# Fused attention and gated feed-forward block: VectorE's order in the ramp written out, a pair of maxima and the filler weights moved, first normalisations by column blocks

## The chip, the cores and the metric

The kernel runs on one core of a Trainium2 chip. The metric is device microseconds of one execution; lower is better. Three executions of the kernel before took 1042.8, 1043.43 and 1046.78 us (median 1043.43).

## The reference

```python
x = A_x                                    # 1 x 2048 x 640, float32
xn = _layernorm(x)                         # (x - mean) / sqrt(var + 1e-5)
qkv = xn @ wqkv                            # 32 heads of 20
scores = q k^T * 20 ** -0.5                # causal, sliding window of 256
attention = softmax(scores) v @ wo
h = gelu(xn @ w_gate) * (xn @ w_up)        # 1728 wide
return x + attention + h @ w_down
```

Matrix products are done in three parts, with each operand split into a high part and the rest (names ending in h and l), to keep float32's precision.

## The kernel before, in words

The 2048 tokens are 16 tiles of 128, taken in four chunks of 512. The program has three stages: a ramp, the attention, and the feed-forward with the output products. The ramp and the first part of the attention are what the change touches.

**The ramp.** For each tile VectorE takes the statistics (`ln_stats`: two halves at L149 and L150, joined at L151). For a group of tiles it then forms the reciprocal root of the variance (`ln_sqrt` and `ln_rstd`: L156 on VectorE, L157 on ScalarE, L162 to L165 on VectorE) and normalises each tile in place (`ln_apply`, L169, one instruction over all 640 columns). TensorE transposes the tiles of a chunk in five column blocks of 128 (`turn`, L185), each into a PSUM bank. ScalarE copies a block as the high part `xh` (L193) and VectorE subtracts that from the bank to give the rest, `xl` (L194). The bank is free again after that. The letters of a string such as "xmxmx" give each block its pool of banks: x is a pool of two, m one of four. A third pool of two, `psd`, holds the projections (tag "dn").

Chunk 0 has its own code, `first_chunk`, in which the order of every engine is the order of the code, since it stands inside `tc.manual_schedule`. It works on two pairs of tiles: statistics, root, normalisation, transposes, copies (L352) and subtractions (L349), then the products with the weights for the first q and k rows (L356). A small copy on GpSimd (`hold`, L370) waits for a pair's last normalised tile, and GpSimd's subtraction for the low weights (L366) stands behind it. The two projections of chunk 0 go out through `save_qk`: ScalarE copies the bank to bf16 (L277), VectorE subtracts (L273, into `r`), ScalarE copies again (L255), GpSimd subtracts (L259), and SyncE stores the three parts to DRAM (L268).

Chunks 1 to 3 are a loop over `c` that follows. There the scheduler of the language orders the engines. `ln_scale` takes the statistics and normalises a chunk's four tiles, `ln_turn` transposes them, and in between lie the products for v (`proj_v`) and the projections of the first q and k rows (`proj_qk`). The activations' tiles `xi` have eight buffers, so the load of a tile waits for the transposes of the tile eight before it.

**The attention.** `attention` is written as slots, 14 to a unit of four heads by 512 queries, with the order of all engines as in the code. Each slot has a few pieces of the work on the unit (scores and exponentials, scores for the maxima, products with v), and a share of filler: the remaining projections and part of the feed-forward, which keep TensorE busy. `pull_max` takes the next pairs of row maxima from a stream that runs ahead of the exponentials: TensorE makes scores in two banks of the m pool (L512), VectorE adds the mask and takes the maximum (L522). Twelve steps ahead of slot 0 belong to the ramp of the attention; there the even ones take two pairs each. In the units slots 0, 5 and 9 take two pairs, slot 0 of later units takes two more, and slot 3 of the first unit two.

SyncE issues nearly all loads and stores and does so in order. `load_stack` loads the q and k stacks of the unit three ahead, the k stack at slot 9 and the q stack at slot 12, in six transfers each (L487). The filler loads its next weights where its own progress asks for them, in `load_qk` (L234) and `load_gu`, two transfers of 320 KB each. `split_later` copies them some fourteen slots later on ScalarE (L656) and makes the low part on GpSimd (L661).

Of the kernel before, what the change touches and what calls it, by code (L numbers as in the profile page):

```python
# [30 lines left out]
NS = 14  # L31
# [36 lines left out]
def block_kernel(ctx, tc, x, wqk, wv, wgu, wdo, wdl, out):  # L68
# [96 lines left out]
        nc.vector.scalar_tensor_tensor(rs, ve, 1.5, rs, op0=OP.add, op1=OP.mult)  # L165
        return rs

    def ln_apply(xi, mv, rs):
        nc.vector.tensor_scalar(xi, xi, mv[:, 0:1], rs, op0=OP.subtract, op1=OP.mult)  # L169

    def ln_scale(xs, lp, mv=None, begun=0):
        n = len(xs)
        mv = mv or lp.tile([128, n, 2], F32, name="mv4", tag="mv4", bufs=2)
        for i in range(begun, n):
            ln_stats(xs[i], mv[:, i, :], lp)
        rs = ln_rstd(*ln_sqrt(mv, n, lp), n, lp)
        for i, xi in enumerate(xs):
            ln_apply(xi, mv[:, i, :], rs[:, i:i + 1])

    def turn(k, xs, where):  # L180
        n = len(xs)
        pool, tag = {"x": (psx, "ex"), "m": (psm, "mx"), "o": (psm, "mx")}[where]
        ps = pool.tile([128, n * 128], F32, name="ps_t", tag=tag)
        for i in range(n):
            nc.tensor.transpose(ps[:, i * 128:(i + 1) * 128], xs[i][:, k * 128:(k + 1) * 128], ident)  # L185
        return ps

    def ln_turn(t0, xs, where="xmxmx"):
        n = len(xs)
        cs = slice(t0 * 128, (t0 + n) * 128)  # L190
        for k in range(KT):
            ps = turn(k, xs, where[k])
            nc.scalar.activation(xh[:, k, cs], ps, AF.Copy)  # L193
            nc.vector.tensor_tensor(out=xl[:, k, cs], in0=ps, in1=xh[:, k, cs].bitcast(F32), op=OP.subtract)  # L194

    acts = {}
    done = set()
# [27 lines left out]
    def behind(fn, *a):  # L225
# [3 lines left out]
        else:  # L229
            fn(*a)  # L230

    def load_qk(t):
        raw = wrp.tile([128, KT, 128], F32, name="wr", tag="wr")
        nc.sync.dma_start(raw, wqk[t])  # L234
        return raw

    def split_qk(raw):
        return split(wp, raw, [128, KT, 128], "wq", nc.gpsimd)
# [106 lines left out]
    def first_chunk(xs, wr0, wr5, prep, v0, lp):  # L345
        halves = slice(0, 256), slice(256, 512)

        def low(k, ps, cs):
            nc.vector.tensor_tensor(out=xl[:, k, cs], in0=ps, in1=xh[:, k, cs].bitcast(F32), op=OP.subtract)  # L349

        def high(k, ps, cs):
            nc.scalar.activation(xh[:, k, cs], ps, AF.Copy)  # L352

        def part(ps, w, r, cs, first=False, last=False, ks=range(KT)):
            for k in ks:
                nc.tensor.matmul(ps[:, cs], w[:, k, :], r[:, k, cs], start=first and k == 0,  # L356
                                 stop=last and k == KT - 1, skip_group_check=True)

        def high_qk(raw):
            wh = wp.tile([128, KT, 128], F32R, name="wqh", tag="wqh")  # L360
            nc.scalar.activation(wh, raw, AF.Copy)
            return wh

        def low_qk(raw, wh):
            wl = wp.tile([128, KT, 128], F32R, name="wql", tag="wql")
            nc.gpsimd.tensor_tensor(out=wl, in0=raw, in1=wh.bitcast(F32), op=OP.subtract)  # L366
            return wh, wl

        def hold(xi):
            nc.gpsimd.tensor_copy(one[:, 0:1], xi[:, 0:1])  # L370

        with tc.manual_schedule(engines=MANUAL | {mybir.EngineType.Pool}):
            mv = [lp.tile([128, 2, 2], F32, name="mv", tag="mv", bufs=2) for _ in range(2)]
# [18 lines left out]
            ln_apply(xs[2], mv[1][:, 0, :], rs[:, 0:1])  # L392
            ln_apply(xs[3], mv[1][:, 1, :], rs[:, 1:2])
# [36 lines left out]
            mv = lp.tile([128, 4, 2], F32, name="mv4", tag="mv4", bufs=2)  # L430
            for j in range(2):
                ln_stats(xs[8 + j], mv[:, j, :], lp)
        save_qk(5, 0, dn[1])
        return w0, w5, v0, mv

    v0 = []
    with tc.tile_pool(name="lp", bufs=1, side="right") as lp:
# [15 lines left out]
        w0, w5, v0, mv = first_chunk(xs, wr0, wr5, prep, v0, lp)  # L453
# [6 lines left out]
        for c in range(1, NC):  # L460
            if c > 1:
                ln_scale(xs[4 * c:4 * c + 4], lp, *((mv, 2) if c == 2 else ()))
            ln_turn(4 * c, xs[4 * c:4 * c + 4], "xmxmx" if c == NC - 1 else "xmxmm")
            if 1 < c < NC - 1:
                xs += [ln_load(t, lp) for t in range(4 * c + 4, 4 * c + 8)]
            if c == 1:
                for i in range(NQ):
                    for j in (0, 2):
                        nc.sync.dma_start(qs[i][SR + 2:64, j:j + 2].rearrange("p j t -> p (j t)"), ones[2:4])
            if c == 2:  # L470
                raws1 = [load_qk(1), load_qk(6)]
            if c < NC - 1:
                run(*[proj_v(v0, 4 * c - 4 + i, None if i % 2 else (psm, "mx")) for i in range(0 if c > 1 else 2, 4)])
                run(proj_qk(0, w0, c), proj_qk(5, w5, c))
# [165 lines left out]
    def load_gu(f):  # L640
        raws = []
        for i in range(2 if f < NF - 1 else 1):
            raw = wrp.tile([128, KT, 128], F32, name="wr", tag="wr")
            nc.sync.dma_start(raw, wgu[2 * f + i])
            raws.append(raw)
        return raws

    def split_gu(pools, raws):
# [174 lines left out]
    def attention():  # L823
# [8 lines left out]
        for i in range(12):  # L832
# [700 lines left out]
```

## Time and profile before

| | us |
|---|---|
| median of three executions | 1043.43 |
| the profiled execution | 1043.06 |
| its span, first to last instruction | 1041.3 |
| TensorE busy | 1031.8 |
| VectorE busy | 740.3 |
| ScalarE busy | 527.9 |
| GpSimd busy | 384.5 |

In the rows, PE is TensorE and PEld its weight loads, DVE is VectorE, ACT ScalarE, POOL GpSimd, and SPq SyncE's queue. L and a number is a line of the kernel before. A row of the timeline has the start, the length, the engine, the line and operation, the tile written and those read, the shape and a count; in brackets stands how long the engine was idle before and what ended that. Neighbouring instructions of one kind are merged in a row, and with matmuls the end of one overlaps the start of the next.

### The profile page before, as it was taken

How to read it: one execution, taken by the hardware profiler on the slowest of the kernel's cores; microseconds unless marked ns; L12 is line 12 of the kernel's file. 1: busy time of each engine (PE TensorE's matmuls, PEld its weight loads, DVE VectorE, ACT ScalarE, POOL GpSimd, SP SyncE). 2: the span in 40 equal slices, each digit the busy share in tenths (PEclk: the TensorE clock that was granted, in tenths of full speed). 3: DMA queues.
4: the chain of work that ended last, by engine and by line, in shares of the span. 5: the costliest groups of instructions: out<-in, count | busy, mean ns of one | idle time of the engine just before them, and what ended most of it. 6: DMA issues, size and time to landing. Idle time of an engine off the chain costs nothing.

```text
span 1041.3 us, 25568 instructions
## 1 busy us (share of the span) xinstructions
PE 1031.8 (99%) x9396; PEld 834.4 (80%) x9396; DVE 740.3 (71%) x2018; ACT 527.9 (51%) x1120; POOL 384.5 (37%) x623
## 2 busy tenths in 40 slices
PE   9999999999999999999999999999999999999998
PEld 8887666666777666666678888888888999999998
DVE  7855666677656576777736778776556888888887
ACT  4434766767666666666675322223324544333332
POOL 5122778988765787766461111101110000000000
PEclk9999999999999999999999999999999999999999
DMA  6642356564633455343325576673117874433333
GB/s 224 182 144 70 110 157 182 160 181 142 185 98 99 117 150 163 94 145 109 99 76 190 187 248 212 246 256 110 72 58 268 252 244 138 137 128 111 127 122 105
DMA packets 102150, 158.74 MB, mean 152 GB/s; under 512 B 14172, under 2 KB 55260, under 8 KB 102024
## 3 DMA queue, kind: packets, MB, share of 16 engines
q1 hardware_dynamic: 99640, 150.94, 45.7%
q10 hardware_dynamic: 2384, 6.16, 1.9%
q8 instruction: 74, 1.21, 0.5%
q14 instruction: 52, 0.43, 0.1%
HBM read 101.78 MB, written 54.92 MB: 150 GB/s over the span
## 4 chain that ended last, share of the span: by engine, by line
PE 92%; DVE 5%; DMA 1%; issue 1%; ACT 1%; SPq 0%; DVEq 0%; ACTq 0%
PE ps_g L977 24%; PE ps L1249 23%; PE ps_d L108 19%; PE ps_e L577 8%; PE ps_v L108 6%; PE ps_o L620 5%; PE ps_m L512 5%; DVE junk L522 2%; PE ps_g L108 1%; PE ps_d L356 1%; DVE xi L169 0%; DMA qs<-qd 0%; PE ps_t L185 0%; DVE st L150 0%; DVE xl L194 0%
## 5 line engine op out<-in xcount | busy, mean ns | idle before, releaser
L522 DVE CUSTOM_DVE_ANT_0 junk<-ps_m,mask 128x320 bf16<-128x320 f32 (+2 forms) x512 | 242.5, 474 | 132.1 <-PE ps_m L512 73.6
L579 ACT ACTIVATE P<-ps_e 128x512 f32<-128x512 f32 (+2 forms) x384 | 198.7, 572 | 65.3 <-PE ps_e L577 64.6
L1249 PE MATMUL ps<-wb,at 128*128 128x320 f32 x999 | 155.9, 309 | 0.0
L1249 PEld LDWEIGHTS ps<-wb,at 128*128 128x128 f32 x999 | 148.9, 188 | 0.2
L592 POOL TENSOR_SCALAR_AFFINE_SELECT P<-P 128x256 f32<-128x256 f32 (+1 forms) x192 | 94.7, 495 | 72.4 <-ACT P L579 71.6
L577 PE MATMUL ps_e<-qs,ks 124*128 124x128 bf16 (+2 forms) x704 | 118.3, 278 | 0.1
L108 PE MATMUL ps_d<-xl,wqh 128*128 128x512 f32 x310 | 98.5, 421 | 0.0
L108 PE MATMUL ps_d<-xh,wqh 128*128 128x512 f32 x310 | 98.3, 421 | 0.0
L108 PE MATMUL ps_d<-xh,wql 128*128 128x512 f32 x310 | 97.6, 418 | 0.0
L101 POOL TENSOR_TENSOR wql<-wr,wqh 128x640 fp32r<-128x640 f32 x12 | 19.2, 1607 | 195.4 <-PE ps_g L977 150.8
L1249 PE MATMUL ps<-wt,at 128*128 128x320 f32 x552 | 88.9, 309 | 0.0
L577 PEld LDWEIGHTS <-ks 124*128 124x128 bf16 x704 | 49.5, 98 | 49.0 <-issue 34.4
L1249 PEld LDWEIGHTS ps<-wt,at 128*128 128x128 f32 x552 | 82.9, 188 | 0.1
L595 POOL TENSOR_SCALAR_AFFINE_SELECT P<-P 128x512 f32<-128x512 f32 (+1 forms) x144 | 76.8, 542 | 16.3 <-ACT P L579 16.3
L1203 ACT ACTIVATE at<-ss 128x512 fp32r<-128x512 f32 x59 | 37.3, 632 | 83.3 <-DVE ss L1082 83.3
L620 PE MATMUL ps_o<-P,v 64*32 64x320 f32 (+4 forms) x2816 | 74.2, 347 | 0.0
L259 POOL TENSOR_TENSOR pt<-r,pt 128x512 bf16<-128x512 f32 x40 | 46.7, 1167 | 64.4 <-ACT pt L255 64.0
L620 PEld LDWEIGHTS ps_o<-P,v 64*32 64x32 f32 x2816 | 50.8, 106 | 21.5 <-issue 0.9
L512 PE MATMUL ps_m<-ks,qs 60*64 60x320 bf16 (+3 forms) x1472 | 64.0, 260 | 3.2 <-DMA qs<-qd 1.1
L108 PEld LDWEIGHTS ps_d<-xh,wql 128*128 128x128 f32 x310 | 56.0, 189 | 10.2 <-issue 1.3
L1006 ACT ACTIVATE hr<-hr 128x512 f32<-128x512 f32 x20 | 12.6, 632 | 101.6 <-DVE hr L980 101.6
L108 PEld LDWEIGHTS ps_d<-xh,wqh 128*128 128x128 f32 x310 | 56.0, 189 | 9.8 <-issue 1.6
(197 smaller groups left out, 1981.6 us busy)
## 6 DMA issues: line engine op xcount, KB each, us to landing
hd<-he SPq DMA_DIRECT2D x50, 256.0 KB
hr<-hd SPq DMA_DIRECT2D x48, 256.0 KB
wr<-wgu SPq DMA_DIRECT2D x27, 320.0 KB
qs<-qd SPq DMA_DIRECT2D x64, 120.0 KB
ks<-kd SPq DMA_DIRECT2D x64, 120.0 KB
xi<-x SPq DMA_DIRECT2D x16, 320.0 KB
qs<-qd SPq DMA_DIRECT2D x64, 80.0 KB
ks<-kd SPq DMA_DIRECT2D x64, 80.0 KB
```

The costliest lines, as they stand in the source:

```text
L108: nc.tensor.matmul(ps, a(k), b(k), start=n == 0, stop=n == 3 * nk - 1)
L259: nc.gpsimd.tensor_tensor(out=pt[:, l, :], in0=r, in1=pt[:, 1, :], op=OP.subtract)
L512: nc.tensor.matmul(ps[64 * h:64 * h + 64, col:col + w], q[rows, j, q0:q0 + 64], ks_, start=True, stop=True, tile_position=(64 * r, 64 * h))
L522: nc.vector.tensor_tensor_reduce(out=junk[:, 0:n], in0=ps[:, 320 - n:320], in1=mask[:, 320 - n:320], scale=1.0, scalar=NEG, op0=OP.add, op ...
L577: nc.tensor.matmul(ps[:, col:col + n], k[0:QROWS, j, kc:kc + 128], q[0:QROWS, j, q0:q0 + n], start=True, stop=True)
L579: nc.scalar.activation(pt[:, j, lo:hi], ps[:, lo:hi], AF.Exp, scale=SCALE)
L592: nc.gpsimd.affine_select(out=a, in_=a, pattern=[[0, n], [1, 128]], compare_op=OP.is_ge, fill=0.0, base=0, channel_multiplier=-1)
L595: nc.gpsimd.affine_select(out=a, in_=a, pattern=[[0, n], [-1, 128]], compare_op=OP.is_ge, fill=0.0, base=-1, channel_multiplier=1)
L620: nc.tensor.matmul(os[r][32 * j:32 * j + 32, qa:qb], v[rows, w0_:w0_ + 32], pt[rows, j, col + qa - q0:col + qb - q0], start=r not in begun ...
L977: nc.tensor.matmul(ps, i, j, start=first and n == 0, stop=n == len(work) - 1, skip_group_check=True)
L1203: nc.scalar.activation(hi[:, 3:7], s, AF.Copy)
L1249: nc.tensor.matmul(ps[bank][:, 0:HD], *work[bank][j], start=bank not in begun, stop=final[p, bank] == n and j == len(work[bank]) - 1, skip ...
```

## The change

It has four parts.

1. *VectorE's order in the ramp.* The loop over chunks 1 to 3 now stands inside a manual schedule for VectorE, and its pieces are put in a written order. The statistics of the first two tiles of the next chunk (`ln_begin`) are taken as soon as a chunk has been normalised. `ln_scale` takes only the other two and follows the transposes of the chunk before. The second projection of chunk 0 leaves in the middle of chunk 1's transposes. The last block of chunk 3's transposes goes to a bank of the projections' pool (letter d) instead of the x pool. Loads move with the pieces: the second of two filler weights ahead of the last four tiles.
2. *A pair of maxima sooner.* Step 11 of the attention's ramp takes two pairs, and slot 3 of the first unit none.
3. *Filler weights behind the q stack.* In slots 5 to 13 of a unit the filler's weight loads are put off to slot 13.
4. *First normalisations by column blocks.* The two pairs of tiles in chunk 0 are normalised in columns 0 to 255 and then 256 to 639: two instructions a tile.

The core of the diff:

```diff
+    def ln_apply(xi, mv, rs, cs=slice(0, D)):
+        nc.vector.tensor_scalar(xi[:, cs], xi[:, cs], mv[:, 0:1], rs, op0=OP.subtract, op1=OP.mult)
+
+    def ln_begin(xs, lp):
+        mv = lp.tile([128, 4, 2], F32, name="mv4", tag="mv4", bufs=2)
+        for i in range(2):
+            ln_stats(xs[i], mv[:, i, :], lp)
+        return mv
...
     def ln_turn(t0, xs, where, mid=None):
...
+            if k == 2 and mid:
+                mid()
...
+    def load_later(src):
+        raw = wrp.tile([128, KT, 128], F32, name="wr", tag="wr")
+        i = 0 if now[0] is None or now[0] < 0 else now[0] % NS
+        if i > 4:
+            at(now[0] + NS - 1 - i, lambda: nc.sync.dma_start(raw, src))
+        else:
+            nc.sync.dma_start(raw, src)
+        return raw
...
-            ln_apply(xs[0], mv[0][:, 0, :], rs[:, 0:1])
-            ln_apply(xs[1], mv[0][:, 1, :], rs[:, 1:2])
+            for cs in (slice(0, 256), slice(256, D)):
+                ln_apply(xs[0], mv[0][:, 0, :], rs[:, 0:1], cs)
+                ln_apply(xs[1], mv[0][:, 1, :], rs[:, 1:2], cs)
...
+            mv = ln_begin(xs[8:], lp)
             save_qk(0, 0, dn[0])
...
+        with tc.manual_schedule(engines={mybir.EngineType.DVE}):
+            for c in range(1, NC):
+                ln_turn(4 * c, xs[4 * c:4 * c + 4], "xmxmd" if c == NC - 1 else "xmxmm",
+                        (lambda: save_qk(5, 0, k_first)) if c == 1 else None)
+                if c == NC - 1:
+                    break
+                ln_scale(xs[4 * c + 4:4 * c + 8], lp, mv)
...
+                run(proj_qk(0, w0, c))
+                if c == 1:
+                    mv = ln_begin(xs[12:], lp)
+                run(proj_qk(5, w5, c))
...
-            elif i % 2 == 0:
+            elif i % 2 == 0 or i == 11:
                 pull_max(2, now[0])
...
-                if i in (0, 5, 9) or T == 3:
+                if i in (0, 5, 9):
                     pull_max(2, T)
```

On VectorE, behind chunk 1's subtractions, the order was this. `mv_556` holds the statistics of chunk 2's tiles, `mv_910` those of chunk 3's, and `xi` written by L169 is a normalised tile of chunk 2.

```order
L156 TENSOR_TENSOR ve<-mv_556,one 128x4
L162 RECIPROCAL rs<-sq 128x4
L151 BN_AGGR mv_910<-st 128x2
L149 BN_STATS st<-xi 128x6
L163 TENSOR_TENSOR ve<-ve,rs 128x4
L150 BN_STATS st<-xi 128x6
L273 TENSOR_TENSOR r<-ps_d,pt 128x512
L164 SCALAR_TENSOR_TENSOR ve<-ve,rs 128x4
L151 BN_AGGR mv_910<-st 128x2
L149 BN_STATS st<-xi 128x6
L165 SCALAR_TENSOR_TENSOR rs<-ve,rs 128x4
L150 BN_STATS st<-xi 128x6
```

In the changed kernel the same place reads as follows; `mv_552` is now chunk 2, `mv_725` chunk 3.

```order
L156 TENSOR_TENSOR ve<-mv_552,one 128x4
L162 RECIPROCAL rs<-sq 128x4
L163 TENSOR_TENSOR ve<-ve,rs 128x4
L164 SCALAR_TENSOR_TENSOR ve<-ve,rs 128x4
L165 SCALAR_TENSOR_TENSOR rs<-ve,rs 128x4
L169 TENSOR_SCALAR xi<-xi,mv_552,rs 128x640 x4
L287 TENSOR_TENSOR r<-ps_d,pt 128x512
L149 BN_STATS st<-xi 128x6
L150 BN_STATS st<-xi 128x6
L151 BN_AGGR mv_725<-st 128x2
```

The steps of the root now follow one another, the four normalisations come right behind them, and the statistics of chunk 3 stand behind the subtraction for `r`.

On SyncE, at slot 12 of unit 4 (counted from 0; the first place in the units where filler weights are loaded, beside the q stack of unit 7), the order was this: `wr` are the weights, `qs` and `ks` the stacks, `qd` and `kd` their stores.

```order
L487 DMA ks_182<-kd_91 60x1024
L234 DMA wr<-wqk 128x640 x2
L268 DMA qd_84<-pt 64x3x512 x2
L487 DMA qs_177<-qd_87 40x1024
L487 DMA qs_177<-qd_87 20x1024
L487 DMA qs_177<-qd_87 60x1024
L487 DMA qs_177<-qd_87 40x1024
L487 DMA qs_177<-qd_87 20x1024
L487 DMA qs_177<-qd_87 60x1024
L268 DMA kd_88<-pt 64x3x512 x2
```

In the changed kernel:

```order
L504 DMA ks_182<-kd_91 60x1024
L282 DMA qd_84<-pt 64x3x512 x2
L504 DMA qs_177<-qd_87 40x1024
L504 DMA qs_177<-qd_87 20x1024
L504 DMA qs_177<-qd_87 60x1024
L504 DMA qs_177<-qd_87 40x1024
L504 DMA qs_177<-qd_87 20x1024
L504 DMA qs_177<-qd_87 60x1024
L243 DMA wr<-wqk 128x640 x2
L282 DMA kd_88<-pt 64x3x512 x2
```

Both weight loads moved past the stores of q and the six loads of the q stack, and stand ahead of the stores of k. The same happens at three later places.

More of the change, by code (lines that the diff above doesn't have):

```diff
@@ L166, in ln_rstd, with ln_scale @@
         return rs
-    def ln_apply(xi, mv, rs):
-        nc.vector.tensor_scalar(xi, xi, mv[:, 0:1], rs, op0=OP.subtract, op1=OP.mult)
-    def ln_scale(xs, lp, mv=None, begun=0):
+    def ln_apply(xi, mv, rs, cs=slice(0, D)):
[5 more added lines that the diff above has]
+        return mv
+    def ln_scale(xs, lp, mv):
         n = len(xs)
-        mv = mv or lp.tile([128, n, 2], F32, name="mv4", tag="mv4", bufs=2)
-        for i in range(begun, n):
+        for i in range(2, n):
             ln_stats(xs[i], mv[:, i, :], lp)
@@ L181, in turn @@
         n = len(xs)
-        pool, tag = {"x": (psx, "ex"), "m": (psm, "mx"), "o": (psm, "mx")}[where]
+        pool, tag = {"x": (psx, "ex"), "m": (psm, "mx"), "o": (psm, "mx"), "d": (psd, "dn")}[where]
         ps = pool.tile([128, n * 128], F32, name="ps_t", tag=tag)
@@ L186, in turn, with ln_turn @@
         return ps
-    def ln_turn(t0, xs, where="xmxmx"):
+    def ln_turn(t0, xs, where, mid=None):
         n = len(xs)
@@ L230, in behind @@
             fn(*a)
+    def load_later(src):
[6 more added lines that the diff above has]
+        return raw
     def load_qk(t):
-        raw = wrp.tile([128, KT, 128], F32, name="wr", tag="wr")
-        nc.sync.dma_start(raw, wqk[t])
-        return raw
+        return load_later(wqk[t])
     def split_qk(raw):
@@ L391, in first_chunk @@
             rs = ln_rstd(*vb, 2, lp)
-            ln_apply(xs[2], mv[1][:, 0, :], rs[:, 0:1])
-            ln_apply(xs[3], mv[1][:, 1, :], rs[:, 1:2])
+            for cs in (slice(0, 256), slice(256, D)):
+                ln_apply(xs[2], mv[1][:, 0, :], rs[:, 0:1], cs)
+                ln_apply(xs[3], mv[1][:, 1, :], rs[:, 1:2], cs)
             hold(xs[3])
@@ L428, in first_chunk @@
                 ln_apply(xs[4 + j], mv[:, j, :], rs[:, j:j + 1])
+            mv = ln_begin(xs[8:], lp)
             save_qk(0, 0, dn[0])
[L430 to L434, printed above, removed]
+        return w0, w5, v0, mv, dn[1]
     v0 = []
@@ L452, in block_kernel @@
         xs += [ln_load(t, lp) for t in range(4, 8)]
-        w0, w5, v0, mv = first_chunk(xs, wr0, wr5, prep, v0, lp)
+        w0, w5, v0, mv, k_first = first_chunk(xs, wr0, wr5, prep, v0, lp)
         ones = lp.tile([4, 2 * C], BF, name="ones")
@@ L459, in block_kernel @@
                 nc.sync.dma_start(ks[i][SR:64, j:j + 2].rearrange("p j t -> p (j t)"), ones)
[L460 to L472, printed above, removed]
+        with tc.manual_schedule(engines={mybir.EngineType.DVE}):
[6 more added lines that the diff above has]
+                if c == 1:
+                    xs += [ln_load(t, lp) for t in range(12, 16)]
+                    for i in range(NQ):
+                        for j in (0, 2):
+                            nc.sync.dma_start(qs[i][SR + 2:64, j:j + 2].rearrange("p j t -> p (j t)"), ones[2:4])
+                else:
+                    raws1 = [load_qk(1), load_qk(6)]
                 run(*[proj_v(v0, 4 * c - 4 + i, None if i % 2 else (psm, "mx")) for i in range(0 if c > 1 else 2, 4)])
-                run(proj_qk(0, w0, c), proj_qk(5, w5, c))
+                run(proj_qk(0, w0, c))
+                if c == 1:
+                    mv = ln_begin(xs[12:], lp)
+                run(proj_qk(5, w5, c))
     vtiles = dict(enumerate(v0[2]))
@@ L642, in load_gu @@
         for i in range(2 if f < NF - 1 else 1):
-            raw = wrp.tile([128, KT, 128], F32, name="wr", tag="wr")
-            nc.sync.dma_start(raw, wgu[2 * f + i])
-            raws.append(raw)
+            raws.append(load_later(wgu[2 * f + i]))
         return raws
```

## The prediction

> **What bounds the kernel now.** The page first: engines, granted clock, and the chain that ended last.
>
> ```profile
> span 1041.3 us, 25568 instructions
> PE 1031.8 (99%) x9396; PEld 834.4 (80%) x9396; DVE 740.3 (71%) x2018; ACT 527.9 (51%) x1120; POOL 384.5 (37%) x623
> ...
> PEclk9999999999999999999999999999999999999999
> ...
> PE 92%; DVE 5%; DMA 1%; issue 1%; ACT 1%; SPq 0%; DVEq 0%; ACTq 0%
> ```
>
> TensorE is busy for 1031.8 of 1041.3 us at full clock, so only the 9.5 us in which it idles can be won, and the diff takes none of its matmuls away. Where those lie is told by busy time in stretches (start:end, length, PE, PEld, DVE, ACT, POOL, clock, DMA) and by the list of TensorE's waits up to 170 us.
>
> ```profile
> 0.00:15.00 15.00, 13.11 (x108) 11.15 (x109) 10.67 (x37) 6.79 (x17) 9.95 (x30) 1.00 0.85 319
> ...
> 150.00:170.00 20.00, 18.58 (x202) 12.07 (x201) 12.64 (x49) 12.64 (x28) 12.88 (x21) 1.00 0.59 174
> ...
> 530.00:1035.00 505.00, 504.89 (x2885) 456.58 (x2885) 385.93 (x737) 195.06 (x353) 37.91 (x33) 1.00 0.50 167
> ```
> ```profile
> PE ps_t L185 <- DVE xi L169: 1.2, 3, 0.8
> ...
> PE ps_m L512 <- DMA qs<-qd: 1.1, 2, 0.6
> PE ps_m L512 <- DVE mx L522: 0.6, 2, 0.4
> ```
>
> The idle time is 1.9 us before 15 and 1.4 between 150 and 170; from 530 to 1035 it is 0.1. The waits name three causes: transposes that wait for normalised rows (VectorE), scores for the maxima that wait for a q stack (DMA), and scores that wait for VectorE's maxima. Each part of the change is aimed at one of these, so I price each by its own rows.
>
> **VectorE's order in the ramp.** Here is the largest single wait: token chunk 2's transposes.
>
> ```profile
> 35.32 1.29 PE L108 MATMUL ps_d<-xh,wql 128*128 128x512 f32 x5
> 36.45 1.29 PE L108 MATMUL ps_d<-xl,wqh 128*128 128x512 f32 x5
> 38.56 2.03 PE L185 MATMUL ps_t<-ident,xi 128*128 128x128 f32 x15 [0.82 <-DVE xi L169]
> ```
> ```profile
> 36.79 0.48 DVE L150 BATCH_NORM_STATS2 st<-xi 128x6 f32<-128x320 f32 x1
> 37.19 2.37 DVE L169 TENSOR_SCALAR xi<-xi,mv,rs 128x640 f32<-128x640 f32 x3
> ```
> ```profile
> 37.00 1.16 POOL L259 TENSOR_TENSOR pt<-r,pt 128x512 bf16<-128x512 f32 x1 [5.54 <-ACT pt L255]
> ```
>
> TensorE finishes the projections at 37.74 and starts at 38.56, because the normalisations began only at 37.19. Statistics of the next chunk's tiles (the row at 36.79 is one) stood among the root's small steps, and three normalisations then took 2.37 beside GpSimd's subtraction. Successive TensorE rows overlap by 0.16 (35.32 + 1.29 is 36.61, the next starts at 36.45), so the loss is 0.82 + 0.16 = 0.98.
>
> In the new order two tiles' statistics move ahead, into an idle stretch, and the normalisations come straight after the root.
>
> ```profile
> 21.29 2.18 DVE L169 TENSOR_SCALAR xi<-xi,mv,rs 128x640 f32<-128x640 f32 x4
> 26.01 0.69 DVE L273 TENSOR_TENSOR r<-ps_d,pt 128x512 f32<-128x512 f32 x1 [2.54 <-issue]
> ```
> ```profile
> 24.86 1.12 ACT L277 ACTIVATE pt<-ps_d 128x512 bf16<-128x512 f32 x2
> 27.27 2.04 ACT L193 ACTIVATE xh<-ps_t 128x512 fp32r<-128x512 f32 x4
> ```
> ```profile
> 7.00 1.14 DVE L169 TENSOR_SCALAR xi<-xi,mv,rs 128x640 f32<-128x640 f32 x2
> ...
> 10.20 0.16 DVE L156 TENSOR_TENSOR ve<-mv,one 128x2 f32<-128x2 f32 x1
> ...
> 11.32 1.41 DVE L169 TENSOR_SCALAR xi<-xi,mv,rs 128x640 f32<-128x640 f32 x2
> 12.65 3.39 DVE L349 TENSOR_TENSOR xl<-ps_t,xh 128x256 fp32r<-128x256 f32 x10
> ```
>
> Two tiles' statistics and the root take what lies between the first two normalisation rows: 7.00 + 1.14 = 8.14 to 11.32, or 3.2. Up to 10.20, where the root begins, it is the statistics; their 2.1 fit into the idle 2.54 ahead of 26.01. ScalarE then sets the pace: eight copies (two of q and k, five xh, one of r) from 24.86 at some 0.55 (half of 1.12; a quarter of 2.04 is 0.51) end at 29.3. VectorE's last xl follows about 1.0 later, at 30.3. Statistics of the other two tiles and the root end at 33.5, and four normalisations (2.18) at 35.7. TensorE asks at 37.58, so about 1.9 us are spare, even behind a second 0.7 lost to GpSimd. **Gain 0.98**; from below 0, if something takes all the spare time.
>
> The statistics of tiles 12 and 13 are now queued ahead of r of the second projection and of chunk 2's xl, some 2 us of VectorE. The first that waits for these is the third product for v, for a bank:
>
> ```profile
> 45.44 0.90 PE L108 MATMUL ps_v<-wvh,xh 128*128 128x320 f32 x5
> ```
>
> It stands 6.9 us behind the transposes at 38.56, so this costs nothing unless tile 13's load is some 4 us late. The last transposes of chunk 3 also go to another bank, and this I cost at nothing, by these two rows:
>
> ```profile
> 58.23 3.19 DVE L194 TENSOR_TENSOR xl<-ps_t,xh 128x512 fp32r<-128x512 f32 x5
> ```
> ```profile
> 60.88 0.31 PE L512 MATMUL ps_m<-ks,qs 60*64 60x64 bf16 x5 [0.18 <-DVE xl L194]
> ```
>
> The second pair of maxima needs the banks of the second and fourth xl. The fourth ends near 58.23 + 3 x 0.63 + 0.67 = 60.79, and 60.88 stays where it is in relation to VectorE. The transposes only come earlier and the pair waits longer; at best 0.2 is won.
>
> **The pair of maxima sooner.** VectorE's rows in the last stretch before slot 0, and TensorE's scores (16 matmuls unhindered, then 16 that wait):
>
> ```profile
> 84.50:89.40 4.90, 4.90 (x44) 4.39 (x42) 0.69 (x1) 2.03 (x7) 1.17 (x1) 1.00 0.28 84
> ```
> ```profile
> 89.08 0.47 PE L512 MATMUL ps_m<-ks,qs 60*64 60x256 bf16 x16
> ```
> ```profile
> 93.50 0.58 PE L512 MATMUL ps_m<-ks,qs 60*64 60x256 bf16 x9
> 94.51 0.33 PE L512 MATMUL ps_m<-ks,qs 60*64 60x128 bf16 x7 [0.43 <-DVE mx L522]
> ```
>
> VectorE works 0.69 of 4.90 us there, then has twelve maxima in a row. The scores of slot 5 take from 93.50 to 94.84, 1.34 instead of 0.47. Two pairs (four maxima) move from slot 3 into the idle stretch, so this wait goes: **gain 0.87**, between 0 (the same wait, earlier, for banks still held by the pairs of step 10) and 0.87. The number of scores and maxima is unchanged.
>
> **Filler weights behind the q stack.** SyncE's queue, its wait, the scores that wait, and the chain:
>
> ```profile
> 157.91 0.86 SPq L234 DMA_DIRECT2D wr<-wqk  x2
> ...
> 160.30 4.74 SPq L487 DMA_DIRECT2D qs<-qd  x6
> ```
> ```profile
> SPq L487 <- DMA wr<-wqk: 2.0, 1, 2.0
> ```
> ```profile
> 166.32 0.27 PE L512 MATMUL ps_m<-ks,qs 60*64 60x256 bf16 x1 [0.60 <-DMA qs<-qd]
> 167.10 0.47 PE L512 MATMUL ps_m<-ks,qs 60*64 60x256 bf16 x15 [0.51 <-DMA qs<-qd]
> ```
> ```profile
> 162.36 4.61 DMA qs<-qd
> ```
>
> The last of six q loads could be issued only once the weights had landed (2.0 us), and the one issued at 162.36 took 4.61 beside them. Here 0.60 is idle and 16 scores take from 166.32 to 167.57, 0.78 more than 0.47: **gain 1.38**. Without the weights' issue (0.86) and the 2.0, the last q load goes out some 2.9 us sooner, more than the 1.38 to be hidden. At the other three places where loads swap, no such wait shows: nothing. What waits now is the weights and the k stores behind them; the first reader is ScalarE:
>
> ```profile
> 172.98 0.75 ACT L656 ACTIVATE wqh<-wr 128x640 fp32r<-128x640 f32 x1
> ```
>
> In the trace the weights landed near 164.7, 6.8 after their issue. Issued near 162 they land by 168.8, with 4 us to spare.
>
> **Normalisations by column blocks.** Each pair of tiles takes four instructions instead of two, and the same columns. What an instruction costs beside its columns follows from two widths of one subtraction:
>
> ```profile
> 41.73 3.08 DVE L194 TENSOR_TENSOR xl<-ps_t,xh 128x512 fp32r<-128x512 f32 x5 [0.18 <-ACT xh L193]
> ```
> ```profile
> 13.11 1.19 PEld L185 LDWEIGHTS ps_t<-ident,xi 128*128 128x128 f32 x8 [0.20 <-DVE xl L349]
> ```
>
> 512 columns come every (3.08 - 0.67) / 4 = 0.60, 256 every (3.39 - 0.41) / 9 = 0.33, which leaves 0.06 per instruction; four more cost 0.25. They stand on the path: second statistics follow the first blocks, the second transposes are paced by the xl of line 349 (the row at 13.11), and these follow the second blocks. The first transposes begin about 0.4 sooner, but the next link, GpSimd's low weights, waits for the whole tile. I take a **loss of 0.25**, between a gain of 0.3 (the earlier start survives) and a loss of 0.64 (0.16 an instruction, the length of the small one at 10.20).
> [...]
>
> **The sum.** 0.98 + 0.87 + 1.38 - 0.25 = 2.98. The profiled execution took 1043.06 (span 1041.3 and 1.8 around it), which gives 1040.1. The median before, 1043.43, is 0.4 above that execution, so I say **1040.2**.
>
> **Rivals.**
> 1. The weights are not what holds the q stack: the stores of q ahead of it are (1.5 us lie between the weights' issue and the first q load, and the stores in it stay). Then 1.38 is lost: 1041.5. Against it stands the 2.0 put down to the weights. 12%.
> 2. The written order moves the wait: ScalarE copies xh later than I reckon, spare time goes, and 0.98 is not won: 1041.1. 12%.
> 3. Column blocks cost 0.16 each: 1040.5. [...]
> 4. The change does more than its rows say (the waits for xl near 59 and 61 shrink as well, the earlier start survives): 1039.3. 5%.
> 5. Slower: the weights land too late for ScalarE's queue, and the exponentials behind the copy at 172.98 wait. This decides from a landing more than 11 us after issue instead of 6.8, at four places. Each must then lose over 0.75 to eat the 2.98; at 13 us it is 2 a place, and 1045. 4%.
>
> My forecast (1039.3 to 1041.0) has 62%. Between 1038.7 and 1043.4 lie all but the slowest case and part of the fourth. A change of 0.5%, about what a measurement of this kernel can tell from no change, is 5.2 us: all the gains together are below that, so faster 3%, within 94%, slower 3%.
>
> **What would show it.** Right: no wait of TensorE for xi near 37 (the normalisations end 1.9 us ahead), none for mx in slot 5, none for qs near 164; TensorE's idle time down by about 2 us. VectorE's xl of line 349 start about 0.25 later than 12.65, and SyncE issues six q loads in about 2.6 us. Wrong: a wait for xl or r in place of the one at 38.56, a wait of ScalarE for wr, or new waits in the steady units, whose order hardly changes.

## The result, and the profile after

| | before | after |
|---|---|---|
| median, us (22 executions each) | 1043.14 | 1041.05 |
| lowest and highest | 1041.62, 1046.78 | 1040.40, 1042.95 |
| the profiled execution | 1043.06 | 1041.63 |
| its span | 1041.3 | 1039.9 |

The ratio is 0.9981, with a 95% interval of 0.9972 to 0.9989: the change wins about 2.0 us. Repeated in a later session it came out smaller, with no gain at all still inside the interval (0.9994, 0.9985 to 1.0003; after_again below). The prediction was 1040.2. In the new rows L529 was L512 before, L539 was L522, L190 was L185, L199 was L194, L363 was L349, L549 was L532, L366 was L352, L370 was L356, L504 was L487, L287 was L273, L282 was L268, L273 was L259. In the rows of only_ramp and ramp_maxima L512 and L522 are L524 and L534, and in those of after_plus1 L512 is L531.

The page of after, engines and chain:

```profile
span 1039.9 us, 25586 instructions
...
PE 1031.0 (99%) x9396; PEld 833.4 (80%) x9396; DVE 742.6 (71%) x2022; ACT 527.5 (51%) x1120; POOL 384.0 (37%) x623
...
PE 94%; DVE 4%; DMA 1%; issue 1%; ACT 0%; SPq 0%; DVEq 0%; ACTq 0%
```

Busy time by stretch, columns as before:

```profile
0.00:15.00 15.00, 11.57 (x103) 9.65 (x104) 10.63 (x39) 6.37 (x15) 10.73 (x30) 1.00 0.85 317
15.00:62.00 47.00, 46.82 (x309) 42.94 (x308) 36.54 (x95) 22.08 (x69) 11.25 (x11) 1.00 0.48 144
...
150.00:170.00 20.00, 19.86 (x209) 12.94 (x206) 14.17 (x54) 13.66 (x30) 14.68 (x24) 1.00 0.62 186
170.00:530.00 360.00, 358.43 (x4888) 246.27 (x4887) 240.18 (x890) 240.02 (x535) 260.69 (x450) 1.00 0.45 132
```

TensorE's idle time between 150 and 170 fell from 1.4 us to 0.1, and up to 15 it rose from 1.9 to 3.4. Its waits, but for the one at the very start and one of 0.2 for xl, which before has too:

```profile
PE ps_t L190 <- DVE xi L169: 0.9, 1, 0.9
PE ps_t L190 <- DVE xl L363: 0.7, 1, 0.7
PE ps_d L370 <- ACT xh L366: 0.5, 1, 0.5
PE ps_m L529 <- DMA qs<-qd: 0.4, 1, 0.4
PE ps_m L529 <- DVE nm L549: 0.2, 1, 0.2
```

The waits for mx are gone, the wait for xi that is left is the very first, and waits for xh (at 11.24) and for xl (at 13.64) and two in the units are new. Totals over the run hide where time comes and goes, so I compared the start of the same TensorE instruction in two traces and call the difference the **lead** over the first profile of before. For example, the first product of wvh with xl behind chunk 2's transposes begins at 41.77 before and at 41.03 after, a lead of 0.74. Leads (us, negative: behind) of every run:

| run | 37 us | 42 | 100 | 163 | 172 | 270 | 620 | end | ratio of times, interval |
|---|---|---|---|---|---|---|---|---|---|
| after | -0.52 | 0.75 | 1.59 | 1.94 | 3.40 | 2.36 | 1.44 | 1.43 | 0.9981 (0.9972, 0.9989) |
| after_again | -0.32 | 0.95 | 1.78 | 2.16 | 3.62 | 3.24 | 2.40 | 1.91 | 0.9994 (0.9985, 1.0003) |
| before_again | -0.21 | -0.80 | -0.80 | -0.80 | 0.66 | 0.69 | 0.67 | 0.51 | 1.0001 (0.9993, 1.0010) |
| only_ramp | 0.15 | 1.42 | 1.37 | 1.38 | 2.84 | 2.56 | 2.17 | 2.17 | 0.9993 (0.9984, 1.0002) |
| only_maxima | 0.14 | 0.14 | 0.98 | 1.34 | 2.73 | 1.52 | 1.44 | 1.29 | 0.9991 (0.9982, 1.0000) |
| only_weights | -0.15 | -0.74 | -0.74 | -0.78 | 0.68 | 0.56 | 0.48 | 0.44 | 1.0000 (0.9992, 1.0009) |
| only_blocks | -0.68 | -0.20 | -0.21 | -0.24 | 0.84 | 0.24 | 0.18 | 0.10 | 1.0004 (0.9995, 1.0013) |
| weights_early | -0.60 | 0.67 | 1.52 | 1.84 | 3.26 | 2.88 | 2.00 | 0.61 | 0.9996 (0.9987, 1.0004) |
| whole_tiles | -0.11 | 1.16 | 2.01 | 2.35 | 3.30 | 3.16 | 2.98 | 2.96 | 0.9972 (0.9962, 0.9983) |
| ramp_maxima | -0.01 | 1.28 | 2.12 | 2.46 | 2.72 | 2.72 | 2.69 | 2.33 | 0.9972 (0.9961, 0.9982) |
| whole_plus4 | 0.04 | 1.31 | 2.15 | 2.49 | 3.95 | 2.85 | 2.01 | 1.79 | 0.9981 (0.9973, 0.9990) |
| whole_plus5 | -0.17 | 1.10 | 1.96 | 2.29 | 3.75 | 3.33 | 3.17 | 3.20 | 0.9975 (0.9966, 0.9985) |
| after_plus1 | -0.64 | 0.63 | 1.46 | 1.80 | 3.26 | 2.98 | 2.88 | 2.91 | 0.9980 (0.9971, 0.9989) |

How to read it: the change's first profile has won 3.40 us by 172, where I had forecast 2.98, and ends with 1.43. So two questions stood after the result: what the gain at 163 to 172 really was, and where 2.0 us went afterwards.

### The profile page after: what moved, and what is told of

Same layout as the page of the kernel before. It is cut to its first block, busy times and chain, and to the rows that moved or that the text cites. A ratio compares the mean times of both kernels' runs of the same rounds, so it can differ in the third digit from the quotient of the medians.

```text
span 1039.9 us, 25586 instructions
## 1 busy us (share of the span) xinstructions
PE 1031.0 (99%) x9396; PEld 833.4 (80%) x9396; DVE 742.6 (71%) x2022; ACT 527.5 (51%) x1120; POOL 384.0 (37%) x623
## 4 chain that ended last, share of the span: by engine, by line
PE 94%; DVE 4%; DMA 1%; issue 1%; ACT 0%; SPq 0%; DVEq 0%; ACTq 0%
PE ps_g L992 24%; PE ps L1264 23%; PE ps_d L108 20%; PE ps_e L594 8%; PE ps_v L108 7%; PE ps_o L637 5%; PE ps_m L529 5%; DVE junk L539 2%; PE ps_g L108 1%; PE ps_t L190 1%; PE ps_d L370 1%; DMA qs<-qd 0%; DVE xi L169 0%; DMA xi<-x 0%; DVE xl L199 0%
## 5 line engine op out<-in xcount | busy, mean ns | idle before, releaser
L539 DVE CUSTOM_DVE_ANT_0 junk<-ps_m,mask 128x320 bf16<-128x320 f32 (+2 forms) x512 | 242.4, 473 | 134.3 <-PE ps_m L529 75.4
L273 POOL TENSOR_TENSOR pt<-r,pt 128x512 bf16<-128x512 f32 x40 | 46.7, 1167 | 64.0 <-ACT pt L269 57.9
L529 PE MATMUL ps_m<-ks,qs 60*64 60x320 bf16 (+3 forms) x1472 | 64.0, 260 | 2.1 <-DMA qs<-qd 0.4
```

The lines of the kernel that those rows point to most:

```text
L273: nc.gpsimd.tensor_tensor(out=pt[:, l, :], in0=r, in1=pt[:, 1, :], op=OP.subtract)
L529: nc.tensor.matmul(ps[64 * h:64 * h + 64, col:col + w], q[rows, j, q0:q0 + 64], ks_, start=True, stop=True, tile_position=(64 * r, 64 * h))
L539: nc.vector.tensor_tensor_reduce(out=junk[:, 0:n], in0=ps[:, 320 - n:320], in1=mask[:, 320 - n:320], scale=1.0, scalar=NEG, op0=OP.add, op ...
```

## The experiments

Each ran in five rounds with the kernel before beside it on the same chip. Intervals are near 0.9 us either way, so single parts are read from the traces, and the times can tell only their larger sums.

**whole_tiles**: the changed kernel without the column blocks.

```diff
-            for cs in (slice(0, 256), slice(256, D)):
-                ln_apply(xs[0], mv[0][:, 0, :], rs[:, 0:1], cs)
-                ln_apply(xs[1], mv[0][:, 1, :], rs[:, 1:2], cs)
+            ln_apply(xs[0], mv[0][:, 0, :], rs[:, 0:1])
+            ln_apply(xs[1], mv[0][:, 1, :], rs[:, 1:2])
```

> The changed kernel with its first four normalisations over whole tiles again; all else as in the changed kernel. Theory (an instruction more costs about 0.19 us, as the pitch 0.325 for 256 columns, 0.39 for 384 and 0.525 for 640 in the changed trace gives; four of them, less what they win at the start, made the first subtraction for xl begin at 13.17 instead of 12.65): the first xl begins near 12.65, TensorE stands 0.5 us ahead of the changed kernel from there to 56 us, and the run ends 0.5 sooner, 1040.5. Rival 1 (0.06 an instruction, as predicted): 0.25 sooner. Rival 2: VectorE sets the end of the ramp in any case, the wait of 0.39 for xl near 60 grows to 0.9, and nothing is won.

Median 1039.44 (ratio 0.9972). VectorE's rows of after, from the first normalisation to the first xl:

```profile
7.05 1.51 DVE L169 TENSOR_SCALAR xi<-xi,mv,rs 128x256 f32<-128x256 f32 x4
8.48 0.49 DVE L149 BATCH_NORM_STATS2 st<-xi 128x6 f32<-128x320 f32 x1
...
11.74 1.52 DVE L169 TENSOR_SCALAR xi<-xi,mv,rs 128x256 f32<-128x256 f32 x4
13.17 0.75 DVE L363 TENSOR_TENSOR xl<-ps_t,xh 128x256 fp32r<-128x256 f32 x2
```

And of whole_tiles:

```profile
7.11 1.14 DVE L169 TENSOR_SCALAR xi<-xi,mv,rs 128x640 f32<-128x640 f32 x2
8.16 0.49 DVE L149 BATCH_NORM_STATS2 st<-xi 128x6 f32<-128x320 f32 x1
...
11.43 1.40 DVE L169 TENSOR_SCALAR xi<-xi,mv,rs 128x640 f32<-128x640 f32 x2
12.76 1.07 DVE L363 TENSOR_TENSOR xl<-ps_t,xh 128x256 fp32r<-128x256 f32 x3
```

From first normalisation to first xl it is 6.12 with blocks and 5.65 whole. In the traces' finer starts it is 6.12 to 6.14 in all five runs with blocks, and 5.64 to 5.65 in all with whole tiles: the blocks cost 0.48, as the theory had it and not the 0.25 of rival 1, and at 163 us whole_tiles is still 0.4 ahead of after, so rival 2 falls too. The first pair takes 1.43 instead of 1.05, 0.19 for each of the two instructions more. But 0.48 at the start does not explain a median that is better by more than one microsecond: whole_tiles also gave back only 0.3 after 172, against 2.0.

**weights_early**: the changed kernel with the weights loaded where they were (`load_later` issues at once).

> The changed kernel with the filler weights loaded where they were before (no putting off to slot 13). Theory (the 3.4 us that the changed trace has won by 171 us were given back to 1.4 because stalls of SyncE's issues, 1 to 2 us each, reach a q stack that is now asked for sooner; the moved weights have nothing to do with it): TensorE is 1.8 us later than in the changed kernel at 171 us, with the two waits for qs near 164 back, the later waits shrink because the stacks have that much more time, and the end is 0.5 to 1.5 later than the changed kernel. Rival (the weights, now behind the q stack, delay the stores and stacks that follow them and so cause the waits at 207 and 264): those waits are gone whole, and the end is 0 to 0.3 later or sooner.

Median 1041.82 (0.9996). The first half of the theory fell: the lead grows by 1.42 between 163 and 172 although the weights stand ahead of the q stack, as it does in after by 1.46. After 172 it loses 1.3 up to 620, and another 1.4 in one wait for `xr` at 832.93. The theory of fixed stalls of SyncE is not borne out either: the places of its waits differ. The waits at 207 and 264 are gone, as the rival had it; but they are gone in after_again too, where the weights stand behind the stack.

**only_weights** and **only_blocks**: the kernel before with one part each, `load_later` or the column blocks.

> The kernel before with nothing changed but the filler weights behind the q stack. Theory: the two waits for qs at 166.32 and 167.10 go, TensorE is 1.8 us (1.4 by the prediction) ahead of the kernel before at 171 us, and of that 0.5 to 1 is given back by 600 us; the end is about 1.0 to 1.4 sooner. Rival 1 (the stores of q hold the stack, not the weights): no gain at 171. Rival 2 (the moved weights make new waits): 1.8 ahead at 171, but a new wait for qs near 207 or 264 and an end within 0.5 of the kernel before.

> The kernel before with nothing changed but the first four normalisations by column blocks. Theory (0.19 an instruction): the first subtraction for xl begins 0.5 later, near 13.2, TensorE is 0.5 behind the kernel before from there to 38 us and keeps it, since VectorE's order behind it follows TensorE's pace; the end is 0.5 later. Rival 1 (0.06 an instruction): 0.25 later. Rival 2: the wait of 0.82 for xi at 38.56 swallows it, and the end is the same.

Medians 1042.45 (1.0000) and 1042.89 (1.0004), against 1042.37 for before. Both gain between 163 and 172, by 1.46 and 1.08, and only one of them has the weights moved. So the wait that I had priced does not come with every execution of the old order. only_blocks is 0.68 behind at 37 and only 0.20 at 42: its wait for chunk 2's normalised rows was shorter and gave back most of the loss, nearer to its rival 2 than to its theory.

**before_again**: the kernel before, unchanged.

> The kernel before once more, unchanged, for a second profiled execution. Theory (SyncE's wait of 2.0 us for the weights, and the two waits of TensorE for the q stack at 166.32 and 167.10, belong to the first execution; three kernels with the same SyncE order at that place stood 1.1 to 1.5 us better there): SyncE issues its six q loads near 160 in under 3.5 us without a wait for weights, and TensorE gains 1.0 to 1.5 on the first profile between 163 and 172 us. Rival (the kernel sets them): both waits recur within 0.3 us.

Median 1042.56 (1.0001). SyncE's q loads, and the scores that had waited:

```profile
160.61 3.49 SPq L487 DMA_DIRECT2D qs<-qd  x6
```
```profile
166.44 0.47 PE L512 MATMUL ps_m<-ks,qs 60*64 60x256 bf16 x16
```

Six loads went out in 3.49 us instead of 4.74, no wait for the weights is listed, and the 16 scores take 0.47. The first profile of the same kernel had lost 1.46 there. The second shows something else at the other place that I had priced, the transposes of chunk 2:

```profile
39.36 1.81 PE L185 MATMUL ps_t<-ident,xi 128*128 128x128 f32 x13 [1.40 <-DVE xi L169]
```
```profile
36.84 0.49 DVE L149 BATCH_NORM_STATS2 st<-xi 128x6 f32<-128x320 f32 x1 [0.18 <-DMA xi<-x]
37.25 1.14 DVE L165 SCALAR_TENSOR_TENSOR rs<-ve,rs 128x4 f32<-128x4 f32 x1
38.31 0.48 DVE L150 BATCH_NORM_STATS2 st<-xi 128x6 f32<-128x320 f32 x1
38.71 0.59 DVE L169 TENSOR_SCALAR xi<-xi,mv,rs 128x640 f32<-128x640 f32 x1
```

This time the last small step of the root stood beside GpSimd's subtraction (37.21 to 38.37) and ended with it, at 38.39: 1.14 us instead of 0.14. In only_weights the same step ended at 38.33 and GpSimd's at 38.31. Tile 13's load also came 0.18 late into the mixed order. The wait is 1.40, not 0.82. only_weights had 1.40 too, only_blocks 0.6, only_maxima 0.8.

**only_ramp** and **only_maxima**: the kernel before with VectorE's written order alone, or with the pair of maxima alone.

> The kernel before with VectorE's written order in the ramp alone (and the bank d, and the loads that move with the pieces); normalisations over whole tiles, maxima and filler weights as before. Theory: no wait for xi near 37, and TensorE is 1.2 us ahead of the kernel before from 42 us on, as in the changed kernel without column blocks (there 0.11 behind at 37 and 1.16 ahead at 42); the end is 1.0 to 1.3 sooner. Rival: the start that is won is eaten by the waits behind it (the scores of slot 5, 0.87), and the end is less than 0.6 sooner.

> The kernel before with only the pair of maxima a step sooner. Theory: the waits for mx near 94 go, TensorE gains 0.85 us between 86 and 100 us and keeps it; the end is 0.8 sooner. Rival: the VectorE work taken sooner delays something else (the scores at 89, or the projection's r), and less than 0.4 is left at 120 us.

Medians 1041.74 (0.9993) and 1041.34 (0.9991). only_ramp gains 1.27 between 37 and 42, as each of the eight other runs with that order does within 0.02; only_maxima gains 0.84 between 42 and 100. only_ramp's rival was wrong: the start that was won stayed. But at 118 only_ramp lost 0.33 again, at this row:

```profile
117.90 0.33 PE L524 MATMUL ps_m<-ks,qs 60*64 60x320 bf16 x3 [0.35 <-DVE mx L534]
```

VectorE had only maxima to do there; more on it below. Near 151 and 155 each kernel with either part gains another 0.35 on the first profile, in two places where the scores of pairs take longer in before; why they do is open.

**ramp_maxima**: the changed kernel without blocks and with the weights loaded early, that is VectorE's order and the maxima alone.

> The changed kernel without the two parts in doubt: whole tiles in the first normalisations, and the filler weights loaded where they were before. It leaves VectorE's order and the pair of maxima. Theory (the wait of SyncE for the weights in the profile of before was that execution's, and the weights' place is worth next to nothing): TensorE is 2.3 us ahead of the kernel before at 163 us, no wait for the landed weights of 2 us recurs, and the median is 1039.4 to 1039.9, within 0.4 of the same kernel with the weights put off (1039.44). Rival (their place is worth the 1.4 us of the prediction): 1040.8.

Median 1039.51, beside 1039.44 for whole_tiles: the place of the weights is worth nothing that a median shows. With the blocks it is the same, by ratio 0.9996 for weights_early and 0.9994 for after_again. The profile of ramp_maxima does have the wait again, in a milder form, and with it a wait of SyncE for the weights, of 0.5 us:

```profile
163.59 0.27 PE L524 MATMUL ps_m<-ks,qs 60*64 60x256 bf16 x1 [0.33 <-DMA qs<-qd]
164.38 0.47 PE L524 MATMUL ps_m<-ks,qs 60*64 60x256 bf16 x15 [0.52 <-DMA qs<-qd]
```

In seven profiles with the weights ahead the loss at this place was 1.46, 0, 0.38, 0.07, 0, 0.04 and 1.20 (1.46 less the growth of the lead from 163 to 172); in seven with the weights behind, 0.51 once and else 0. The means differ by 0.4, but the 1.46 comes from the profile in which I had found the wait; without it the six others with the weights ahead have 0.28 on the mean and the seven behind 0.07. That the part makes this wait rarer is likely but not shown, and waits for q stacks further on, which also come and go, would hide it.

**after_again**: the changed kernel once more.

> The changed kernel once more, unchanged, for a second profiled execution and for times on one chip with the others. Theory (the waits behind 171 us in its first profile, 0.51 before the scores at 206.79, 0.72 at 263.99 and smaller ones, hang on when a transfer happened to land and belong to that execution): up to 163 us TensorE stands as in the first profile within 0.15 us, about 1.9 ahead of the kernel before; the waits at 207 and 264 are not both there, others may be. Rival (they are set by the kernel): both recur, within 0.2 us, and the span is 1039.9 again.

Median 1041.86 (0.9994). Two waits of the first profile, at 207 and at 264 (after, then after_again):

```profile
206.79 0.47 PE L529 MATMUL ps_m<-ks,qs 60*64 60x256 bf16 x15 [0.22 <-DVE nm L549]
...
263.99 0.47 PE L529 MATMUL ps_m<-ks,qs 60*64 60x256 bf16 x15 [0.43 <-DMA qs<-qd]
```
```profile
206.07 0.47 PE L529 MATMUL ps_m<-ks,qs 60*64 60x256 bf16 x16
...
263.09 0.47 PE L529 MATMUL ps_m<-ks,qs 60*64 60x256 bf16 x16
```

They did not recur. For the wait at 206.79 the profile names VectorE's `nm`, but that cannot be all: in after_again `nm` ended at 206.51 and the scores had begun at 206.07, and in after a transfer of the q stack landed at 206.66. Up to 163 us after_again stood 0.22 ahead of the first profile, not within 0.15; 0.20 of it lies ahead of 37 us. But three smaller losses did recur, in after, after_again and weights_early alike and in no kernel with whole tiles so far: 0.27 near 288, 0.27 near 429 and 0.11 near 562. only_blocks, whose VectorE stream is three instructions shorter, has none of them. In after_again, TensorE and then VectorE at the first of them:

```profile
286.92 0.76 PE L529 MATMUL ps_m<-ks,qs 60*64 60x320 bf16 x8
```
```profile
285.81 0.49 DVE L539 CUSTOM_DVE_ANT_0 junk<-ps_m,mask 128x320 bf16<-128x320 f32 x1
286.23 0.08 DVE L539 DVE_READ_ACCUMULATOR2_ANT mx<- 128x1 f32 x1
286.80 0.49 DVE L539 CUSTOM_DVE_ANT_0 junk<-ps_m,mask 128x320 bf16<-128x320 f32 x1 [0.49 <-DVE mx L539]
287.22 0.08 DVE L539 DVE_READ_ACCUMULATOR2_ANT mx<- 128x1 f32 x1
287.44 0.49 DVE L539 CUSTOM_DVE_ANT_0 junk<-ps_m,mask 128x320 bf16<-128x320 f32 x1
```

Behind one read of a maximum the next maximum begins after 0.57 us, behind the following one after the usual 0.22. Nothing else was awaited: the releaser named is VectorE's own read, long done. I counted the instructions of VectorE's stream from 0, those that only wait included. Such longer gaps stand, among others, at numbers 191, 575, 959 and 1471 in after_again, 191, 447, 703 and 1215 in before, 319 (the 118 us of only_ramp) and 1343 in only_ramp, 1087 in whole_tiles: 63 and a multiple of 128. Over all 14 traces, a maximum that follows a read of a maximum (with at most a waiting instruction between) stands at such a number 54 times, and all 54 have the gap (0.57 to 0.61). The few other gaps of about that length, such as the one before 245.75 in before, are waits for TensorE's scores. In whole_tiles number 959 is a read, 0.42 behind its maximum as all reads are, and the pair near 287 is not delayed. So what the column blocks did at 288 might only be that they are four instructions more. The last three runs test this.

**whole_plus4**, **whole_plus5** and **after_plus1**: small instructions at the very start of VectorE's stream, in idle time (four or five on top of whole_tiles, one on top of after).

```diff
         nc.vector.memset(warm, 0.0)
+        for _ in range(4):
+            nc.vector.memset(spare[:, 0:8], 0.0)
```

> The changed kernel with whole tiles in the first normalisations, and four small VectorE instructions (memsets of a spare tile) at the very start, before the first rows of x have landed. Theory (in every trace so far the time between two maxima that follow one another is 0.35 us longer at the same numbers of VectorE's stream, 191, 447, 575, 703, 959, 1087, 1215, 1343, 1471 and so on, 128 apart, whenever a maximum begins there; which maxima these are shifts with the count of instructions ahead, and the column blocks add four): the ramp is that of the whole tiles, but the longer gaps now stand near 77, 183, 287 and 429 us as in the changed kernel, TensorE waits 0.27 for maxima near 287.5 and 429, and the end is 0.5 to 0.7 later than with whole tiles alone. Rival (these waits come from the column blocks or from when the ramp ends): none of them, and the same end as with whole tiles alone.

> The same with five small instructions instead of four. Theory: with five, none of the numbers 63 + 128 n falls on a maximum that follows another at once, so no gap between such maxima is longer, the waits near 287 and 429 are gone, and the end is that of the whole tiles alone (0 to 0.1 apart in the trace up to 520 us). Rival (the added instructions cost something by themselves): it loses as much as four, or more.

> The changed kernel, column blocks and all, with one small VectorE instruction more at the start. Theory: with five more than the whole tiles in all, the waits for maxima near 288 and 430 and the longer gaps go, and the run ends 0.5 to 0.6 sooner than the changed kernel, though it has an instruction more; the loss of 0.49 in the ramp stays. Rival (the waits come from the column blocks): they stay, and the end is that of the changed kernel or later.

The scores of the pairs near 287 and 429, TensorE, first whole_plus4, then whole_plus5, then after_plus1:

```profile
287.33 0.76 PE L529 MATMUL ps_m<-ks,qs 60*64 60x320 bf16 x8
...
429.07 0.77 PE L529 MATMUL ps_m<-ks,qs 60*64 60x320 bf16 x8
```
```profile
286.85 0.47 PE L529 MATMUL ps_m<-ks,qs 60*64 60x320 bf16 x8
...
428.30 0.47 PE L529 MATMUL ps_m<-ks,qs 60*64 60x320 bf16 x8
```
```profile
287.17 0.47 PE L531 MATMUL ps_m<-ks,qs 60*64 60x320 bf16 x8
...
428.65 0.47 PE L531 MATMUL ps_m<-ks,qs 60*64 60x320 bf16 x8
```

The scores of a pair take 0.76 where they wait for a delayed maximum, and else 0.47. Four more instructions bring the delays into a kernel without blocks; five do not; one more takes them out of the kernel with blocks. The 0.11 near 562 follows them. Medians: 1040.19 with four and 1039.69 with five; none of the 11 executions with four took less than 1040.05, and seven of the nine with five did. after_plus1 took 1040.22, ratio 0.9980 against 0.9994 for after_again: the theory had 0.5 to 0.6 for this, and the traces show 0.65, so the rest of the difference is one-off waits and scatter. whole_plus5 ended 0.2 better in its trace than whole_tiles; each of the two has a one-off wait of about 0.45 at the scores of a pair, at another place (at 234.87, where the profile names `nm`, and at 163.81, where it names a q stack), so I call them equal. The theory of the numbers holds, and its rivals fall.

whole_tiles, ramp_maxima and whole_plus5 (1039.4 to 1039.7, ratios 0.9972 to 0.9975) come out below both kernels, though their intervals overlap that of the first measurement of after (0.9981). The shortest way to most of it is to leave the changed kernel's column blocks out.

## Why the time came out right and the steps did not

The time, 1041.05, lies 0.85 above the forecast: 0.05 above the forecast's own upper bound of 1041.0, and inside the wider 1038.7 to 1043.4. Rival 2 gave 1041.1, almost the time measured, by a mechanism that did not happen, since the 0.98 was won. That the time fits is partly luck, as the terms show:

- **VectorE's order: 0.98 forecast, 1.27 measured** against the first profile, and 1.86 against the second (1.27, and 0.59 that before_again itself lost from 37 to 42). The mechanism was right. These are the rows of after:

```profile
38.11 2.35 PE L190 MATMUL ps_t<-ident,xi 128*128 128x128 f32 x20
40.21 0.98 PE L108 MATMUL ps_v<-wvh,xh 128*128 128x320 f32 x5
```
```profile
33.93 2.18 DVE L169 TENSOR_SCALAR xi<-xi,mv,rs 128x640 f32<-128x640 f32 x4
36.03 0.68 DVE L287 TENSOR_TENSOR r<-ps_d,pt 128x512 f32<-128x512 f32 x1
```

  The normalisations end at 36.1 (I had worked out 35.7, and the start came 0.5 later), 2.0 ahead of the transposes. The sum had left out the fourth tile, whose transposes stood apart in before:

```profile
40.35 0.54 PE L108 MATMUL ps_v<-wvh,xh 128*128 128x320 f32 x2
40.73 0.77 PE L185 MATMUL ps_t<-ident,xi 128*128 128x128 f32 x5
41.25 0.69 PE L108 MATMUL ps_v<-wvh,xh 128*128 128x320 f32 x3
```

  From the first transpose to the first product of wvh with xl it was 3.21 us before (38.56 to 41.77) and is 2.92 now (38.11 to 41.03), with all 20 transposes in one piece: the other 0.29. And the wait was not a constant: in the mixed order it differs from run to run, 0.6 to 1.4 us, with what stands beside GpSimd's subtraction and with the landing of tile 13's load. The bank d gave nothing, as said: TensorE still waits 0.2 for xl at 60.

- **The pair of maxima: 0.87 forecast, 0.84 measured** (only_maxima). Right. The scores of slot 5 stand in after as they should:

```profile
92.83 0.47 PE L529 MATMUL ps_m<-ks,qs 60*64 60x256 bf16 x16
```

- **The filler weights: 1.38 forecast, nothing to be seen in the times.** This is the step that failed: it took a wait of one execution for one of the kernel. Each of its rows was true of that execution: SyncE did wait 2.0 for the weights and TensorE did lose 1.4. But the same program, run again, did not. Rival 1 said that the weights were not what held the stack; nearer the truth is that nothing holds it every time. The signs that I named prove nothing. No wait for qs near 164 came true, but in four of the six other profiles with the weights ahead the loss there was also below 0.1. The six loads took 2.97 us here instead of the 2.6 forecast, and 3.24 to 3.79 in the other six profiles with the weights behind, against 3.28 to 3.62 in the six others with the weights ahead.

- **The column blocks: 0.25 lost by the forecast, 0.48 measured in the ramp** (the first xl at 13.17 instead of 12.65 in the first profiles), and 0.65 more by the numbers of the stream. The step that failed was to take the fixed cost from another operation. The subtraction for xl reads a bank and takes 0.60 for 512 columns and 0.33 for 256, so 0.06 is fixed. The normalisation takes 0.53 for 640, 0.39 for 384 and 0.325 for 256 (starts of successive instructions in the trace of after): half as much for a column (0.53 ns against 1.05), and 0.19 fixed. That is two instructions more in the first pair, 0.38. The second pair costs 0.10 only (1.43 with blocks, 1.33 whole): with whole tiles its first instruction, at 11.32 in before, stood beside a memset of GpSimd (10.92 to 11.86) and took 0.81 instead of 0.53; with blocks it began at 11.74, when that memset (10.91 to 11.85) was all but over. Rival 3, which I gave 5%, had this with 0.16 each.

So against a profile without the one-off wait the sum is 1.27 + 0.84 + 0.35 (near 151 and 155, which no step had) - 0.48 - 0.65 = 1.33, or 1.92 with the longer wait of before_again in the ramp. The two measured differences, 2.0 and 0.7 by their ratios, lie on either side of these. The forecast's 2.98 was too high: 1.38 that is not there and 0.88 too little for the blocks, set off in part by 0.6 to 1.2 too little for the rest. What it did foresee is the size: all gains together stay below 0.5%. One sum among the rivals is wrong as it stands: in rival 5 four places of 2 us make 8, and about 1048 instead of 1045. No wait of ScalarE for the moved weights is listed in after.

Of what I had named as signs of being wrong, one came: new waits in the steady units. 0.65 of them is fixed (288, 429, 562). The other 1.3 in the first profile of after is waits such as those at 207 and 264; the second profile has neither, but loses about 1.1 at other places. Which transfer or releaser makes these q stacks late in one execution and not in the next is open. So is what happens at numbers 63 + 128 n: the rows show the gap there, 0.57 to 0.61 us from a read to the next maximum instead of 0.22, and none shows what makes it.

## What to carry to other kernels

Before you price a wait that a DMA's landing ends, look at a second profile of the same kernel: of the two waits that made up most of this forecast, one cost anything from nothing to 1.5 us and the other 0.6 to 1.4. Take the fixed cost of splitting an instruction from two widths of that same instruction (0.06 by the subtraction here, 0.19 by the normalisation itself). And when adding or removing a few instructions moves waits far away in unchanged code, count their places in the engine's stream and try one instruction more before looking for a cause in the data.

## What the runs showed of the hardware

- In these traces a maximum that follows a read of a maximum began 0.57 to 0.61 us behind it instead of 0.22 wherever it stood at a number 63 + 128 n of VectorE's stream: 54 places in 12 of the 14 traces; whole_plus5 and after_plus1 have no such place. Near 287 and 429 us this cost TensorE 0.27 each or nothing, by the count of instructions ahead of it; one memset of 128 x 8 took 0.65 us of waits out in after_plus1.
- A VectorE instruction of 128 x 4 elements took 1.14 us instead of 0.14 beside GpSimd's 1.16 us subtraction and ended within 0.02 of it (before_again); in another execution of the same program the long one was a normalisation (1.32 instead of 0.60, in before).
